# A hashed attention with a max-out FFN behind it: the first batch cut into thirds of its queries, values by even and odd dimensions of four heads, scaling straight out of PSUM, and one list of PSUM banks

## The chip, the cores and the metric

The kernel runs on one core of a Trainium2 chip. The metric is the time of one execution in microseconds of the device (us); smaller is better. One execution was also taken by the hardware profiler, and all views of the profile come from that one.

## What is computed

Four batches of eight heads, 768 positions, 64 dimensions. Each query and key gets a bucket of six bits (the signs of six projections); a query attends only to the keys of its own bucket. The heads' outputs side by side are the 512 columns of `x`, which goes through three matrices, a maximum, and a fourth matrix.

```python
q_bits = (einsum('bhsd,dk->bhsk', q, proj) > 0)          # k the same
mask = q_bucket[:, :, :, None] == k_bucket[:, :, None, :]
scores = where(mask, q @ k.T / sqrt(64), -1e9)
attn = exp(scores - max); attn = attn / (sum(attn) + 1e-9)
x = (attn @ v).transpose(0, 2, 1, 3).reshape(3072, 512)
h = maximum(maximum(x @ w1, x @ w2), x @ w3)             # 512 -> 768
out = h @ w_out                                          # 768 -> 512
```

## The kernel before

The bits stand as extra rows (plus or minus a half) under the 64 rows of each transposed head in a tile `S`, so that one matmul over 70 or 72 rows gives the score with the mask in it, and exp with a bias gives nearly zero where buckets differ.

A *unit* is 768 columns of scores: two matmuls of 128 keys by 384 queries (`scores`, L255) into one of two PSUM buffers, and one exp on ScalarE (L257) into one of 18 tiles `AT`. There are 192 units, 48 a batch. Six units make one head for one half of the queries. The program is one loop over units `u`, written out by hand, and every engine works through its own queue in that order: scores of unit u+1, then what the table `at` holds for u (`when(u, ...)`: preparation of later heads, loads), then one group of the FFN if one is waiting, then values and sums that are due.

- Preparation of batch 0 goes by *pairs* of heads. Loads of four pairs go out at the start on SP. For each pair there are four transposes on TensorE (`pair_turn`, L111), four copies to SBUF on VectorE (`pair_keep`, L117), four placings into `S` on GpSimd (`pair_place`, L122), one hash (`pair_hash`, L133: eight matmuls in fp32), the bits on VectorE (L137), and four small DMAs on SP that put the bits under the heads (L142), two a head. Pair 0 has its own shorter way (`first_place`, `first_hash`, `first_bits`: L147, L153, L158). Pairs 1 to 3 are turned at units 1 to 4, 8 to 15 and 17 to 20, and needed at units 12, 24 and 30.
- Later batches go by *quads* of four heads, turned by VectorE (L176), narrowed by GpSimd (L181), placed and hashed by L187 to L207.
- Values (`values`, L281): for a group of two heads and half of the queries, 24 matmuls of 32 columns of V, four side by side in the four 32-column strips of the array, 385 columns of `AT` each (the last is a column of ones, for the sum of V). Six such rounds fill one bank of its own. Sums (L308, L337) are the same with ones as weights.
- `far` copies the bank to SBUF (`avs`, L330), makes the reciprocals (L291 to L294), spreads them over partitions by GpSimd copies (L343 to L347), and scales six units later (L351). `near` scales out of PSUM (L314), for two groups of batch 0.
- FFN of a half of the queries: 18 first-layer groups of four matmuls (L366; L370 and L372 on VectorE) and six second-layer groups (L399, L403), one group a unit. The halves of batch 0 enter at units 40 and 57.
- PSUM: two score buffers of two banks, one bank for values, three for everything else. Weights and V are loaded by GpSimd's DMA queue: w1, w2, w3 and w_out at units 1, 9, 22 and 30, V of quad 1 at unit 14.

Of the kernel before, what the change touches and what calls it, by code (L numbers as in the profile page):

```python
# [17 lines left out]
def kernel(  # L18
# [12 lines left out]
    nc = tc.nc  # L31
# [9 lines left out]
    NPAIR = B * HPAIR  # L41
# [5 lines left out]
    UPG = NM  # L47
# [5 lines left out]
    NAT = 18  # L53
    LAG = 1

# [8 lines left out]
    avs_pool = ctx.enter_context(tc.tile_pool(name="avspool", bufs=5))  # L64
# [6 lines left out]
    av_ps = ctx.enter_context(tc.tile_pool(name="av_ps", bufs=1, space=bass.MemoryType.PSUM))  # L71
    ms_ps = ctx.enter_context(tc.tile_pool(name="ms_ps", bufs=3, space=bass.MemoryType.PSUM))
# [7 lines left out]
    at_tiles = [konst.tile([P, 2, HALF + 2], FP16, name=f"AT{i}", tag=f"AT{i}") for i in range(NAT)]  # L80
# [3 lines left out]


# [22 lines left out]
    def pair_turn(pi, side, hd, mp):  # L108
        n = nat[pi].rearrange("p (s h w) -> p s h w", s=2, h=2)
        for i in range(MH):  # L110
            nc.tensor.transpose(mp[:, i * P : (i + 1) * P], n[:, side, hd, i * P : (i + 1) * P], iden[:])  # L111
        return mp

    def pair_keep(pi, side, hd, mp):
        if pi not in t32:
            t32[pi] = t32_pool.tile([P, 2, S], FP32, tag="T32", name="T32")
        nc.vector.tensor_copy(t32[pi][:, side, hd * HALF : (hd + 1) * HALF], mp[:, 0:HALF])  # L117
# [6 lines left out]
    def pair_group(pi, side, hd):  # L124
        mp = ms_ps.tile([P, 512], FP32, tag="ms", name="mp")
        pair_keep(pi, side, hd, pair_turn(pi, side, hd, mp))

    def pair_hash(pi):
        bp = ms_ps.tile([P, 512], FP32, tag="ms", name="bp")
        for side in (1, 0):  # L130
            for hd in range(2):
# [3 lines left out]
        t32.pop(pi)  # L135
        bits = b_pool.tile([P, HALF], BF16, tag="bits", name="bits")
        nc.vector.tensor_scalar(out=bits[:], in0=bp[:, 0:HALF], scalar1=0.0, scalar2=0.5,  # L137
                                op0=AluOp.is_gt, op1=AluOp.subtract)
        for hd in range(2):
            for side in (1, 0):  # L140
                g = 2 * side + hd
                nc.sync.dma_start(s_of[pi][D : D + NBITS, g, :].rearrange("b (c n) -> b c n", c=2),  # L142
                                  bits[Q * g : Q * g + 2 * NBITS, :])
# [40 lines left out]

# [4 lines left out]

    def quad_hash(g):  # L190
        bp = ms_ps.tile([P, 512], FP32, tag="ms", name="bp")
        ts = [t32.pop((side, g)) for side in range(2)]
        for u in range(2):
            for side in range(2):
                for j in range(2):
# [5 lines left out]
                                op0=AluOp.is_gt, op1=AluOp.subtract)  # L201

# [9 lines left out]
    def v_tile(g):  # L212
        t = vo_pool.tile([P, 4, NM * D], FP16, tag="vo", name="vo")
        for x in range(4):
            v_at[4 * g + x] = (t, x)
        return t

    def load_v(g):
        b, h0 = divmod(4 * g, H)
        nc.gpsimd.dma_start(v_tile(g)[:], v[b, h0 : h0 + 4].rearrange("h (p c) d -> p h (c d)", p=P))  # L220

    def load_weights(i):
        t, w = ((w_sb[0], moe_w1), (w_sb[1], moe_w2), (w_sb[2], moe_w3), (wout_sb, moe_w_out))[i]
        nc.gpsimd.dma_start(t[:], w.rearrange("(c p) f -> p c f", p=P))


    groups = [(b, qh, jj) for b in range(B) for qh in range(2) for jj in range(HPAIR)]
    groups[0:8] = [(0, g % 2, g // 2) for g in range(4)] + [(0, g // 2, 2 + g % 2) for g in range(4)]
    NU = len(groups) * UPG
    UPB = NU // B  # L230
    xts, avs_of, av_of, sm_of = {}, {}, {}, {}


    def unit_of(u):
        g, n = divmod(u, UPG)
        if g < 4:
            hd, n = divmod(u % (2 * UPG), UPG)
            return 2 * (g // 2) + n // MH, hd, n % MH
        return g, n // MH, n % MH

    def place_of(g, hd, kp):
        if g < 4:
            return (g // 2) * 2 * UPG + hd * UPG + (g % 2) * MH + kp
        return g * UPG + hd * MH + kp

    def scores(u):
        g, hd, kp = unit_of(u)
        b, qh, jj = groups[g]
        hh = b * H + 2 * jj + hd
        (qn, qx), (kn, kx) = where[0, hh], where[1, hh]  # L250
        nb = NBITS if b == 0 else KB
        sc = sc_ps.tile([P, 2, 512], FP32, tag="sc", name="sc")
        for j in range(2):
            m = 2 * kp + j
            nc.tensor.matmul(sc[:, j, 0:HALF], s_of[kn][0 : D + nb, kx, m * P : (m + 1) * P],  # L255
                             s_of[qn][0 : D + nb, qx, qh * HALF : (qh + 1) * HALF], start=True, stop=True)
        nc.scalar.activation(at_tiles[u % NAT][:, :, 0:HALF], sc[:, :, 0:HALF], ActFn.Exp,  # L257
                             bias=-SCALE * 0.25 * nb, scale=SCALE)

    def xt_of(g):  # L260
        b, qh, jj = groups[g]
        h = 2 * b + qh
        if h not in xts:
            xts[h] = x_pool.tile([P, NJC, HALF], FP16, tag="xT", name="xT")
        return xts[h][:, jj, :]

    def at_of(g, m, hd):
        return at_tiles[place_of(g, hd, m // 2) % NAT][:, m % 2, :]

# [3 lines left out]
    def values(g):  # L273
        b, qh, jj = groups[g]
        av = av_ps.tile([P, 512], FP32, tag="av", name="av")
        for m in range(NM):
            for hd in range(2):
                vt, x = v_at[b * H + 2 * jj + hd]
                c = block_of(b, m)
                for w in range(2):  # L280
                    nc.tensor.matmul(av[hd * D + w * Q : hd * D + (w + 1) * Q, 0 : HALF + 1],  # L281
                                     vt[:, x, c * D + w * Q : c * D + (w + 1) * Q],
                                     at_of(g, m, hd)[:, 0 : HALF + 1], start=(m == 0), stop=(m == NM - 1))
        return av

    def inverse(o, sm):
        ys = ys_pool.tile([P, HALF], FP32, tag="ys", name="ys")
        rr = small.tile([P, HALF // Q], FP32, tag="rr", name="rr")  # L290
        nc.vector.transpose(ys[:], sm[:, 0:HALF])  # L291
        nc.vector.tensor_scalar(out=rr[:], in0=ys[:, 0:HALF:Q], scalar1=EPS * S, scalar2=None, op0=AluOp.add)
        nc.vector.reciprocal(rr[:], rr[:])
        nc.vector.transpose(o, rr[:].unsqueeze(2).to_broadcast((P, HALF // Q, Q)))  # L294


    def near(g):
        avs = []

        def part_values():  # L300
            avs.append(values(g))

        def part_sums():
            av = avs[0]
            sm = ms_ps.tile([P, 512], FP32, tag="ms", name="sm")
            for m in range(NM):
                for r in range(4):
                    nc.tensor.matmul(sm[Q * r : Q * (r + 1), 0:HALF], ones[:, :], at_of(g, m, r // 2)[:, 0:HALF],  # L308
                                     start=(m == 0), stop=(m == NM - 1))
            sv = small.tile([P, 2], FP32, tag="sv", name="sv")  # L310
            rc = rb_pool.tile([P, 2, HALF], FP32, tag="rb", name="rb")
            inverse(rc[:, 0, :], sm)
            nc.vector.tensor_scalar(out=sv[:, 0:1], in0=av[:, HALF : HALF + 1], scalar1=EPS, scalar2=None, op0=AluOp.mult)
            nc.vector.scalar_tensor_tensor(out=xt_of(g), in0=av[:, 0:HALF], scalar=sv[:, 0:1], in1=rc[:, 0, :],  # L314
                                           op0=AluOp.add, op1=AluOp.mult)

        return part_values, part_sums


    def far(gs):  # L320
        avs, sms, sb = [], [], []

        def part_values(i):
            if not sb:
                sb.append(small.tile([P, 2], FP32, tag="sv", name="sv"))
                sb.append(rb_pool.tile([P, 2, HALF], FP32, tag="rb", name="rb"))
            sv = sb[0]
            av = values(gs[i])
            avs.append(avs_pool.tile([P, HALF + 4], FP32, tag="avs", name="avs"))
            nc.vector.tensor_copy(avs[i][:, 0 : HALF + 1], av[:, 0 : HALF + 1])  # L330
            nc.gpsimd.tensor_scalar_mul(sv[:, i : i + 1], avs[i][:, HALF : HALF + 1], EPS)  # L331

        def part_sums():
            sms.append(ms_ps.tile([P, 512], FP32, tag="ms", name="sm"))
            for m in range(NM):
                for r in range(4):
                    nc.tensor.matmul(sms[0][Q * r : Q * (r + 1), 0:HALF], ones[:, :],  # L337
                                     at_of(gs[r % 2], m, r // 2)[:, 0:HALF], start=(m == 0), stop=(m == NM - 1))

        def invert():  # L340
            rb = sb[1]
            inverse(rb[:, 0, :], sms[0])
            nc.gpsimd.tensor_copy(rb[:, 1, :], rb[:, 0, :])  # L343
            for p0 in (0, D):
                nc.gpsimd.tensor_copy(rb[p0 + Q : p0 + D, 0, :], rb[p0 : p0 + Q, 0, :])  # L345
            for p0 in (0, D):
# [260 lines left out]
```

## Time and profile before

| | |
|---|---|
| median of three runs | 283.51 us (282.56 to 285.82) |
| span of the profiled execution | 280.6 us (its time outside the span is not recorded) |
| TensorE, weight loads, VectorE, ScalarE, GpSimd busy | 270.2, 145.9, 177.3, 166.2, 106.9 us |
| granted TensorE clock, mean | 0.998 |
| first scores, first FFN matmul, end of the last matmul | 8.5, 52.6, 277.1 us |

A group line of the profile reads: line, engine, operation, tiles, shapes, count, then busy time and mean duration in ns. A matmul's duration holds its passage through the array; how fast matmuls follow one another is read from their starts. A line of the time line reads: start, length, engine, line, what, count, and in brackets how long the engine was idle before and what ended that. A line by stretch reads: from, to, length, then the busy time (and count) of TensorE, its weight loads, VectorE, ScalarE, GpSimd, the granted clock, the share of the DMA engines and GB/s.

### The profile page before, as it was taken

What the parts mean: (1) busy time and instruction counts of PE and PEld (TensorE: products, weight loads), DVE (VectorE), ACT (ScalarE), POOL (GpSimd) and SP (SyncE); (2) the same over time, 40 slices, a digit from 0 to 9 for tenths busy, and PEclk for the clock granted to TensorE, in tenths of its full rate; (3) what the DMA queues carried; (4) which work ended last, traced back from release to release, by engine and by line L of the source; (5) the groups of instructions that cost most, each with busy time, mean ns of one, the idle gap of its engine ahead of it and who ended that gap; (6) DMA issues with size and microseconds to landing.
All of it is one profiled execution on the core that took longest, in us unless ns stands there. A gap on an engine that the chain in (4) does not pass through costs nothing.

```text
span 280.6 us, 6405 instructions
## 1 busy us (share of the span) xinstructions
PE 270.2 (96%) x2482; PEld 145.9 (52%) x2482; DVE 177.3 (63%) x383; ACT 166.2 (59%) x220; POOL 106.9 (38%) x201
## 2 busy tenths in 40 slices
PE   8899989899999999999999999999999999999994
PEld 4344433454555554555555554555555555555552
DVE  3755786786536594796536594896536673568580
ACT  2686676763858484764858484864858485910102
POOL 3455958153119096543118096633021120303000
PEclk9999999999999999999999999999999999999999
DMA  7998879974117439672117349772020001200303
GB/s 231 320 183 165 127 133 230 245 101 105 42 42 200 101 50 232 180 148 70 30 70 183 85 67 225 206 122 63 1 77 37 2 1 40 75 2 0 114 0 112
DMA packets 21877, 30.99 MB, mean 110 GB/s; under 512 B 2632, under 2 KB 17368, under 8 KB 21848
## 3 DMA queue, kind: packets, MB, share of 16 engines
q0 software_dynamic: 8640, 12.59, 24.9%
q1 hardware_dynamic: 12776, 17.49, 21.7%
q10 hardware_dynamic: 432, 0.52, 0.6%
q8 instruction: 19, 0.31, 0.5%
q14 instruction: 10, 0.08, 0.1%
HBM read 25.17 MB, written 6.29 MB: 112 GB/s over the span
## 4 chain that ended last, share of the span: by engine, by line
PE 87%; DVE 6%; ACT 2%; issue 2%; DMA 1%; POOL 0%; DVEq 0%; ACTq 0%
PE l L366 31%; PE sc L255 21%; PE av L281 12%; PE l L399 10%; PE sm L337 5%; PE bp L197 3%; ACT AT L257 2%; PE mp L111 2%; PE wp L438 1%; DVE ht L372 1%; PE bp L133 1%; PE bp L153 1%; PE sm L308 1%; DMA out_dram<-osb 1%; DVE rb L294 1%
## 5 line engine op out<-in xcount | busy, mean ns | idle before, releaser
L257 ACT ACTIVATE AT<-sc 128x768 f16<-128x768 f32 x192 | 153.4, 813 | 78.2 <-PE sc L255 78.0
L366 PE MATMUL l<-xT,w_sb 128*128 128x384 f16 x576 | 113.2, 326 | 0.7 <-DVE ht L372 0.6
L255 PE MATMUL sc<-S 72*128 72x384 bf16 (+1 forms) x384 | 93.1, 326 | 3.8 <-ACT AT L257 3.0
L366 PEld LDWEIGHTS <-w_sb 128*128 128x128 f16 x576 | 55.9, 97 | 39.1 <-issue 1.2
L372 DVE TENSOR_TENSOR ht<-ht,l 128x384 f16<-128x384 f16 x96 | 52.4, 546 | 17.0 <-PE l L366 13.8
L255 PEld LDWEIGHTS <-S 72*128 72x128 bf16 (+1 forms) x384 | 35.0, 98 | 40.1 <-issue 15.6
L331 POOL TENSOR_SCALAR sv<-avs 128x1 f32<-128x1 f32 x30 | 6.4, 213 | 95.8 <-DVE avs L330 95.7
L330 DVE COPY avs<-av 128x385 f32<-128x385 f32 x30 | 16.8, 560 | 38.3 <-PE av L281 38.3
L281 PE MATMUL av<-AT,vo 128*32 128x385 f16 x768 | 37.3, 327 | 0.0
L399 PE MATMUL l<-wout_sb,ht 128*128 128x512 f16 x138 | 36.5, 379 | 0.4 <-DVE ht L372 0.4
L370 DVE CAST ht<-l 128x384 f16<-128x384 f32 x48 | 26.2, 547 | 16.0 <-PE l L366 15.2
L403 ACT COPY osb<-l 128x512 f32<-128x512 f32 x23 | 13.4, 582 | 27.2 <-PE l L399 27.2
L281 PEld LDWEIGHTS <-vo 128*32 128x32 f16 x768 | 18.6, 96 | 16.9 <-issue 8.7
L181 POOL TENSOR_SCALAR T<-T 128x768 bf16<-128x768 f32 x24 | 21.5, 894 | 13.3 <-DVE T L176 11.9
L176 DVE STREAM_TRANSPOSE T<-nat 128x384 f32<-128x384 f32 x48 | 26.2, 558 | 0.0
L399 PEld LDWEIGHTS <-ht 128*128 128x128 f16 x138 | 13.3, 97 | 13.8 <-DVE ht L372 1.8
L351 DVE SCALAR_TENSOR_TENSOR xT<-avs,sv,rb 128x384 f16<-128x384 f32 x30 | 19.7, 656 | 0.0
L337 PE MATMUL sm<-AT,ones 128*32 128x384 f16 x360 | 17.2, 326 | 0.0
L343 POOL COPY rb<-rb 128x384 f32<-128x384 f32 x15 | 7.5, 503 | 24.0 <-DVE rb L294 24.0
L122 POOL TENSOR_SCALAR S<-T 64x768 bf16<-64x768 f32 (+1 forms) x17 | 12.8, 754 | 8.0 <-DVE T L117 6.9
L347 POOL COPY rb<-rb 32x384 f32<-32x384 f32 x30 | 15.0, 500 | 1.5
L345 POOL COPY rb<-rb 32x384 f32<-32x384 f32 x30 | 15.0, 499 | 1.5
(47 smaller groups left out, 136.5 us busy)
## 6 DMA issues: line engine op xcount, KB each, us to landing
out_dram<-osb SPq DMA_DIRECT2D x23, 256.0 KB
S<-T SPq DMA_DIRECT2D x48, 96.0 KB
vo<-in_v_dram POOLq DMA_DIRECT2D x8, 384.0 KB, 6.1
nat<-in_k_dram POOLq DMA_DIRECT2D x16, 192.0 KB, 3.6
nat<-in_q_dram POOLq DMA_DIRECT2D x16, 192.0 KB, 5.8
w_sb<-in_moe_w_dram POOLq DMA_DIRECT2D x3, 768.0 KB, 9.7
nat<-in_k_dram SPq DMA_DIRECT2D x10, 192.0 KB
nat<-in_q_dram SPq DMA_DIRECT2D x8, 192.0 KB
```

The source lines that it names most:

```text
L176: nc.vector.transpose(t32[name][:, u, half * HALF : (half + 1) * HALF], i_)
L181: nc.gpsimd.tensor_scalar(out=t16[name][:, u, :], in0=t32[name][:, u, :], scalar1=RS, scalar2=1.0, op0=AluOp.mult, op1=AluOp.mult)
L255: nc.tensor.matmul(sc[:, j, 0:HALF], s_of[kn][0 : D + nb, kx, m * P : (m + 1) * P], s_of[qn][0 : D + nb, qx, qh * HALF : (qh + 1) * HALF], ...
L257: nc.scalar.activation(at_tiles[u % NAT][:, :, 0:HALF], sc[:, :, 0:HALF], ActFn.Exp, bias=-SCALE * 0.25 * nb, scale=SCALE)
L281: nc.tensor.matmul(av[hd * D + w * Q : hd * D + (w + 1) * Q, 0 : HALF + 1], vt[:, x, c * D + w * Q : c * D + (w + 1) * Q], at_of(g, m, hd) ...
L330: nc.vector.tensor_copy(avs[i][:, 0 : HALF + 1], av[:, 0 : HALF + 1])
L337: nc.tensor.matmul(sms[0][Q * r : Q * (r + 1), 0:HALF], ones[:, :], at_of(gs[r % 2], m, r // 2)[:, 0:HALF], start=(m == 0), stop=(m == NM ...
L351: nc.vector.scalar_tensor_tensor(out=xt_of(gs[i]), in0=avs[i][:, 0:HALF], scalar=sv[:, i : i + 1], in1=rb[:, i, :], op0=AluOp.add, op1=Alu ...
L366: nc.tensor.matmul(ps[:, 0:HALF], w_sb[wi][:, jc, fb * P : (fb + 1) * P], xt[:, jc, :], start=(jc == 0), stop=(jc == NJC - 1))
L370: nc.vector.tensor_copy(hts[fb][:], ps[:, 0:HALF])
L372: nc.vector.tensor_tensor(out=hts[fb][:], in0=hts[fb][:], in1=ps[:, 0:HALF], op=AluOp.max)
L399: nc.tensor.matmul(ps[:, 0:DM], hts[fb][:, tb * P : (tb + 1) * P], wout_sb[:, fb, :], start=(fb == 0), stop=(fb == NFB - 1))
```

## The change

- **Thirds.** Batch 0 is cut into three chunks of 256 queries; the other batches keep two of 384. A unit of a third is three matmuls of 128 keys by 256 queries, and a head has two such units. The order starts with heads 0 and 1 in chunks 0 and 1, then heads 2 to 7 of chunk 0, heads 2 to 7 of chunk 1, then chunk 2. So head 2 (pair 1) comes at unit 8, pair 2 at unit 12, pair 3 at unit 16. Turns of pairs 1 to 3 are set at units 1 to 3, 4 to 7 and 8 to 11, hashes at 4, 8 and 12; the second half of each pair's queries is placed later (units 10, 14, 18).
- **Values.** A burst is four heads of one chunk: one bank of sums, one of even dimensions, one of odd ones, 24 matmuls each. Its value weights are every second element of V. The rows of w1, w2 and w3 are loaded in an order that fits.
- **Scaling** reads PSUM, with the reciprocals already in the right partitions; the avs copies and the GpSimd copies go. The sum of V is taken once for each quad and side.
- **Banks.** Four banks in one list, taken and given back in order. There are 26 AT tiles.
- **Order.** Bursts of chunks 0 to 2 are split over three units, the others are in one piece; quad hashes come one unit later, outside the burst. FFN of a chunk enters two units after its last piece: chunk 0 at unit 24. Chunk 0's FFN goes matrix by matrix. The loads of w1, w2, w3 and w_out are at units 0, 7, 11 and 28, V of quad 1 at unit 5; the keys of quad 2 are loaded at unit 9 and no longer at the start. Two of pair 0's copies go from VectorE to ScalarE.

```diff
-    groups = [(b, qh, jj) for b in range(B) for qh in range(2) for jj in range(HPAIR)]
...
+    chunks = [(b, w * n, w) for b in range(B) for w in (THIRD if b == 0 else HALF,)
+              for n in range(S // w)]
...
+    order = [(0, 0), (1, 0), (0, 1), (1, 1)] + [(c, h) for c in range(2) for h in range(2, H)]
+    order += [(c, h) for c in range(2, NCH) for h in range(H)]
...
+            for m in range(m0, m1):
+                cb = block_of(b, m)
+                for x in range(4):
+                    nc.tensor.matmul(av[Q * x : Q * (x + 1), 0:n], v_at[2 * b + i][:, x, cb * D + side : (cb + 1) * D : 2],
+                                     weights_of(c, 4 * i + x, m)[:, 0:n], start=(m == 0), stop=(m == NM - 1))
...
+                nc.vector.scalar_tensor_tensor(out=xt_of(c)[:, 2 * i + side, 0:w], in0=av[:, 0:w],
+                                               scalar=sv_of[b, i, side][:], in1=rb[0][:, 0:w], op0=AluOp.add, op1=AluOp.mult)
...
+        if c == 0:
+            jobs = [(fb, wi) for wi in range(3) for fb in range(NFB)]
...
-        load_quad(1, 2, range(4), nc.sync)
...
+        pair_keep(0, 1, 1, mk1, nc.scalar)
...
-        for pi, us, uh in ((1, (1, 2, 3, 4), 6), (2, (8, 9, 14, 15), 16), (3, (17, 18, 19, 20), 21)):
+        for pi, us, uh, ul in ((1, (1, 1, 2, 3), 4, 10), (2, (4, 5, 6, 7), 8, 14), (3, (8, 9, 10, 11), 12, 18)):
             for u, (side, hd) in zip(us, ((1, 0), (1, 1), (0, 0), (0, 1))):
                 when(u, pair_group, pi, side, hd)
                 if hd == 1:
-                    for par in range(2):
-                        when(u, pair_place, pi, side, par)
+                    when(u, pair_place, pi, side, 0)
+                    when(u if side == 1 else ul, pair_place, pi, side, 1)
             when(uh, pair_hash, pi)
-        when(14, load_v, 1)
-        for n, u in enumerate((1, 9, 22, 30)):
+        when(5, load_v, 1)
+        for n, u in enumerate((0, 7, 11, 28)):
             when(u, load_weights, n)
-        for u, side, g in ((8, 0, 2), (23, 1, 3), (25, 0, 3)):
+        for u, side, g in ((9, 1, 2), (12, 0, 2), (23, 1, 3), (25, 0, 3)):
...
+            for n, f in enumerate(pieces):
+                u = d + n if c < 3 else d
...
+            ffn_at.setdefault(last_of[c] + 2, []).append(c)
```

More of the change, by code (lines that the diff above doesn't have):

```diff
@@ L241, in place_of @@
[L241 to L268, printed above, removed]
+        if i == 3:
+            nc.gpsimd.dma_start(wout_sb[:], moe_w_out.rearrange("(c p) f -> p c f", p=P))
+            return
+        w = (moe_w1, moe_w2, moe_w3)[i]
+        nc.gpsimd.dma_start(w_sb[i].rearrange("p (i u) f -> p i (u f)", u=2),
+                            w.rearrange("(i p u) f -> p i (u f)", p=P, u=2))
@@ new lines, with parts_of @@
+    chunks = [(b, w * n, w) for b in range(B) for w in (THIRD if b == 0 else HALF,)
+              for n in range(S // w)]
+    NCH = len(chunks)
+    def parts_of(c):
+        return chunks[c][2] * NM // (2 * HALF)
+    order = [(0, 0), (1, 0), (0, 1), (1, 1)] + [(c, h) for c in range(2) for h in range(2, H)]
+    order += [(c, h) for c in range(2, NCH) for h in range(H)]
+    units = [(c, h, n) for c, h in order for n in range(parts_of(c))]
+    NU = len(units)
+    UPB = NU // B
+    done_at = {}
@@ L270, in block_of, with blocks @@
+    for u, (c, h, n) in enumerate(units):
+        done_at[c, h // 4] = u
+    at_free = list(range(NAT))
+    at_form = [THIRD] * NAT
+    at_of = {}
+    xts, sv_of = {}, {}
+    def blocks(t, w):
+        nb = 2 * HALF // w
+        return t[:, 0 : nb * (w + 2)].rearrange("p (n c) -> p n c", n=nb)
     def block_of(b, m):
         return 2 * (m % MH) + m // MH if b == 0 else m
[L273 to L284, printed above, removed]
@@ L288, in inverse @@
[L288 to L308, printed above, removed]
-                                     start=(m == 0), stop=(m == NM - 1))
[L310 to L317, printed above, removed]
@@ L320, in far @@
[L320 to L346, printed above, removed]
-                nc.gpsimd.tensor_copy(rb[p0 : p0 + Q, 1, :], rb[p0 + Q : p0 + D, 1, :])
-        def scale(i):
-            sv, rb = sb
-            nc.vector.scalar_tensor_tensor(out=xt_of(gs[i]), in0=avs[i][:, 0:HALF], scalar=sv[:, i : i + 1],
-                                           in1=rb[:, i, :], op0=AluOp.add, op1=AluOp.mult)
-        return part_values, part_sums, invert, [(6 + i, lambda i=i: scale(i)) for i in range(2)]
@@ new lines, with weights_of, xt_of, burst @@
+    unit_at = {e: u for u, e in enumerate(units)}
+    def weights_of(c, h, m):
+        w = chunks[c][2]
+        nb = 2 * HALF // w
+        return blocks(at_tiles[at_of[unit_at[c, h, m // nb]]], w)[:, m % nb, :]
+    def xt_of(c):
+        if c not in xts:
+            xts[c] = x_pool.tile([P, NJC, HALF], FP16, tag="xT", name="xT")
+        return xts[c]
+    def burst(c, i):
+        b, q0, w = chunks[c]
+        held = {}
+        rb = []
+        def sums(m0, m1):
+            if m0 == 0:
+                held["s"] = bank()
+            sm = held["s"][1]
+            for m in range(m0, m1):
+                for x in range(4):
+                    nc.tensor.matmul(sm[Q * x : Q * (x + 1), 0:w], ones[:, :], weights_of(c, 4 * i + x, m)[:, 0:w],
+                                     start=(m == 0), stop=(m == NM - 1))
+            if m1 == NM:
+                ys = ys_pool.tile([P, HALF], FP32, tag="ys", name="ys")
+                rr = small.tile([P, HALF // Q], FP32, tag="rr", name="rr")
+                n = w // Q
+                rb.append(rb_pool.tile([P, HALF], FP32, tag="rb", name="rb"))
+                nc.vector.transpose(ys[:, 0:w], sm[:, 0:w])
+                give(held["s"][0])
+                nc.vector.tensor_scalar(out=rr[:, 0:n], in0=ys[:, 0:w:Q], scalar1=EPS * S, scalar2=None, op0=AluOp.add)
+                nc.vector.reciprocal(rr[:, 0:n], rr[:, 0:n])
+                nc.vector.transpose(rb[0][:, 0:w], rr[:, 0:n].unsqueeze(2).to_broadcast((P, n, Q)))
+        def values(side, m0, m1):
+            if m0 == 0:
+                held[side] = bank()
+            av = held[side][1]
+            first = (b, i, side) not in sv_of
+            n = w + 1 if first else w
+            for m in range(m0, m1):
+                cb = block_of(b, m)
+                for x in range(4):
+                    nc.tensor.matmul(av[Q * x : Q * (x + 1), 0:n], v_at[2 * b + i][:, x, cb * D + side : (cb + 1) * D : 2],
+                                     weights_of(c, 4 * i + x, m)[:, 0:n], start=(m == 0), stop=(m == NM - 1))
+            if m1 == NM:
+                if first:
+                    sv_of[b, i, side] = small.tile([P, 1], FP32, tag=f"sv{side}", name="sv")
+                    nc.vector.tensor_scalar(out=sv_of[b, i, side][:], in0=av[:, w : w + 1], scalar1=EPS, scalar2=None,
+                                            op0=AluOp.mult)
+                nc.vector.scalar_tensor_tensor(out=xt_of(c)[:, 2 * i + side, 0:w], in0=av[:, 0:w],
+                                               scalar=sv_of[b, i, side][:], in1=rb[0][:, 0:w], op0=AluOp.add, op1=AluOp.mult)
+                give(held[side][0])
+                if side == 1:
+                    for h in range(4 * i, 4 * i + 4):
+                        for n in range(parts_of(c)):
+                            at_free.append(at_of[unit_at[c, h, n]])
+        return sums, values
@@ new lines, in ffn_groups, with go @@
+    def ffn_groups(c):
+        b, q0, w = chunks[c]
+        xt = xt_of(c)
+        hts, gs, l2 = {}, [], {}
+        jobs = [(fb, wi) for fb in range(NFB) for wi in range(3)]
+        if c == 0:
+            jobs = [(fb, wi) for wi in range(3) for fb in range(NFB)]
+        for fb, wi in jobs:
+            def go(fb=fb, wi=wi):
+                k_, ps = bank()
+                for jc in range(NJC):
+                    nc.tensor.matmul(ps[:, 0:w], w_sb[wi][:, jc, fb * P : (fb + 1) * P], xt[:, jc, 0:w],
+                                     start=(jc == 0), stop=(jc == NJC - 1))
+                if wi == 0:
+                    hts[fb] = h_pool.tile([P, HALF], FP16, tag="ht", name="ht")
+                    nc.vector.tensor_copy(hts[fb][:, 0:w], ps[:, 0:w])
+                else:
+                    nc.vector.tensor_tensor(out=hts[fb][:, 0:w], in0=hts[fb][:, 0:w], in1=ps[:, 0:w], op=AluOp.max)
+                give(k_)
+            gs.append(go)
```

248 lines of the change are left out of this document (118 added, 130 removed).

## The prediction

> **What bounds the kernel now.** I read the page first (busy shares, slices, chain), then the stretches of time, then the time line of the first 45 us, because the slices are uneven only there.
>
> ```profile
> PE 270.2 (96%) x2482; PEld 145.9 (52%) x2482; DVE 177.3 (63%) x383; ACT 166.2 (59%) x220; POOL 106.9 (38%) x201
> ...
> DMA  7998879974117439672117349772020001200303
> ...
> PE 87%; DVE 6%; ACT 2%; issue 2%; DMA 1%; POOL 0%; DVEq 0%; ACTq 0%
> ```
>
> TensorE is the bound and the chain runs along it; VectorE and GpSimd have room. Two lines by stretch show where TensorE is not full:
>
> ```profile
> 30.00:40.00 10.00, 8.98 (x104) 3.67 (x101) 7.08 (x15) 6.61 (x10) 6.35 (x9) 1.00 0.70 96
> ...
> 62.00:100.00 38.00, 38.00 (x374) 20.71 (x372) 21.73 (x45) 23.94 (x32) 12.28 (x27) 1.00 0.39 96
> ```
>
> The second number is TensorE's busy time. From 62 us on it is full, and the starts of its matmuls confirm it: 0.162 us apart for 384 columns, which is one L366 group of four in 0.65. Adding up the gaps between starts that exceed this, I find 7.0 us of waiting between 8.5 us (first scores) and 52.6 us (first FFN matmul), and about 1 us in all after that. So the span is a start of 52.6 us, then 224.5 us of nearly solid matmuls up to 277.1, then 3.6 us of copying out. What the change does to time is the start, plus the work left after it.
>
> In the start the heads are made ready by a long path: transpose (PE, L111), copy (DVE, L117), hash (PE, L133), bits (DVE, L137), four small DMAs on SP (L142).
>
> ```profile
> 16.44 0.85 PE L133 MATMUL bp<-T,pj 128*32 128x384 f32 x8
> ...
> 17.41 0.56 DVE L137 TENSOR_SCALAR bits<-bp 128x384 bf16<-128x384 f32 x1 [1.35 <-PE bp L133]
> ...
> 18.00 3.29 SPq L142 DMA_DIRECT2D S<-bits  x4
> ```
>
> That is pair 1 (heads 2, 3). By the trace's DMA records the two transfers of head 2 landed at 20.2 and 20.9, 4.5 us after the hash began. Head 2 is unit 12, whose exp ran at 21.6: just in time. Now the last bits of pair 3 against a weight load:
>
> ```profile
> 35.53 0.79 POOL L224 DMA_DIRECT2D w_sb<-in_moe_w_dram  x1
> ```
>
> ```profile
> 28.64 8.34 SPq L142 DMA_DIRECT2D S<-bits  x8
> ```
>
> The eight issues of the second line (0.72 each) are pairs 2 and 3. Those issued at 33.96 and 34.73 landed after 1.9 us. The one issued at 36.26, 0.73 behind the weight load, landed at 42.5, with the tail of that load (42.2 to 43.4); its packets last 0.05 us each but the first starts at 40.9. Likewise the bits issued at 29.43, just behind the load of V at 28.96, landed at 34.5 with it. Small transfers issued behind a large load land with its end.
>
> **The change, part by part.**
>
> *Work left after the first FFN matmul*, priced by spacings of this trace (0.162 for 384 columns; 0.109 for 256, from the twelve matmuls of L381: 1.47 us less the 0.27 of one, over 11). FFN of chunk 0 starts at u24, with scores up to 25 done, where before it started at u40 with scores up to 41 done.
> - Scores left: 66 of 256 columns and 288 of 384 against 300: 7.2 + 46.5 - 48.5 = +5.2.
> - First layer of batch 0: 216 x 0.109 - 144 x 0.162 = +0.3.
> - Values left: four quads of 12 rounds (a round is four matmuls side by side) at 0.109 against 12 rounds at 0.162: +3.3. Sums: 24 rounds at 0.109 against 6 at 0.162: +1.6.
> - One more quad hash is left (1.4), and four hashes leave the middle of a burst and pay the switch in and out again (0.2 each): +2.2. The gap on going into 32-column matmuls is 0.095 us and out again 0.098; batch 0 has 12 separate pieces left against 3: +1.7.
> - The wait at 251.8 us for a late scale (0.8) goes, since PSUM is scaled at once: -0.8. Next on VectorE there: transpose 0.58, two small ones 0.40, transpose 0.58, two scalings of 0.62; three banks are held for that 2.8 us, while TensorE still has the two value pieces (1.9) and two groups on the other banks. No new wait.
> - VectorE at u24 to u31: a transpose (0.56), an evacuation of 256 columns (0.42, L387) and 2.0 of burst work twice in four units make about 9.8 us against 8.7 of TensorE: +1.0 (0 to 2).
>
> Sum: +14.5, so 224.5 + 14.5 = 239.0. The removed avs copies (L330, 16.8 us) and GpSimd's rb and sv copies (L331 to L347, 44 us) lie beside a full TensorE; I price them at nothing, and their cover is TensorE itself. The added memsets (0.06 each) and the wider value weights with a step of two elements lie there too.
>
> Rounds of 256 columns are not in the trace. Lower end 0.109: the weight loads of a round are issued with the round before and take 0.097, so they still fit. Upper end 0.162, if the round does not shrink: 72 rounds, +3.8. I take the lower, as L381 has the same weight loads and gets 0.109.
>
> *The start.* Batch 0 needs pair 1 at u8 instead of u12, pair 2 at u12 instead of u24, pair 3 at u16 instead of u30. TensorE's queue is in order: while scores(8) waits for bits, the transposes of the next pair wait behind it, and ACT and the next hash behind those.
> - Pair 1: two copies of the first pair move to ACT (0.5 each, beside its 0.57 of waiting after the first exp). On DVE, eight small bits (0.56) from 7.3, then four copies (0.55) end at 15.1; hash at 15.2, bits at 16.2, SP at 16.75. Head 2's second transfer is issued at 17.7 and lands 1.9 later: scores(8) at 19.7. (w1 is out at about 11.6, and the four k loads of quad 2, taken out of its way, were 2.6 us of packets, so it is drained by then.)
> - Pair 2: its last transpose stands behind scores(8): 20.4, copy to 21.15, hash 21.2, bits 22.2 to 22.7, SP 22.75 and 23.7. But GpSimd's queue runs from the same copy: place (L122, 0.86) to 22.0, then w2 at 22.05. V of quad 1 went out at 19.6. So the bits stand 0.7 us behind a weight load, as at 36.26. With 7.0 us from the load's issue to the landing of such bits (42.5 - 35.5), scores(12) run at 29.1, instead of 25.7 with 1.9.
> - Pair 3 repeats it: copy ends 1.5 after scores(12), place, w3 at 31.4, bits behind it (k loads of quad 2 now stand between in SP's queue, 2.3 us of issues over by 28): landing 38.4, scores(16) at 38.5. The burst of the first quad lies in that wait.
> - From scores(16), four units at ACT's 0.75, then three of scores, burst piece and switch (0.33 + 0.65 + 0.19 = 1.17), and the lag to scores(25): 8.0. First FFN matmul at 46.5. Weights are in by then; w_out goes out near 50, took 11.9 us before, and is needed near 66.
>
> **Sum.** 46.5 + 239.0 + 3.6 = 289.1 us of span, against 280.6. The median of the runs shown, 283.5, is 2.9 above the profiled span, and I add the same: 292.0. In other words the start gives back 6.1 us and 14.5 us of work are still to do, since TensorE waits some 14 us in the start instead of 7.
>
> [...] The row says that the bits of 36.26 waited 4.7 us for their first packet. [...]
>
> **The rivals.**
> 1. *The bits slip past the loads* (1.9 us as at 33.96). scores(12) at 25.7, pair 3's bits issued at 29.7 land at 31.6, first FFN at 39.7: span 282.3, time 285.2. For it: the order of the w2 issue and the bits rests on 0.7 us of my walk. Against it: two loads, both ahead by the same construction.
> 2. *Faster.* The pairs are ready before TensorE asks, so that ACT alone sets the pace: 24 units at 0.75 to 0.8 from 9.0, and four burst pieces that exceed it by 0.4, plus the tiny waits of the first units (1.3 at units 0 to 4 instead of 0.8): first FFN at 34 to 35. Span 277.1, time 280.0. It turns on one thing, scores(12) not waiting; below a first FFN at 35.2 the change is faster by 1%. Against it: hash to landing took 4.5 us, and four units of ACT are 3.0.
> 3. *Rounds of 256 columns do not shrink*: +3.8 on the sum, 295.8. For it: eight instructions in 0.109 us occur nowhere. Against: the four matmuls of a round start within 10 ns.
> 4. *Only one of the two pairs is caught*: first FFN near 43, 288.5.
>
> The clock is a further unknown. The warm-up matmuls took 0.320 instead of 0.162 for the first 4 us of the run, and later no gap of TensorE reaches 1.3 us; here it idles for over 4 us before scores(12). [...]
>
> **How the numbers follow.** Likeliest, both caught: 0.42, own range 289 to 294. Rival 1: 0.23. Rival 2: 0.12. Rival 3 on top of the likeliest: 0.13. Rival 4: 0.10. The range goes from the fast side of rival 1 (first FFN at 36.5) to rival 3: 282 to 296; rival 2 and a little above are left out. One per cent of 283.5, about what a measurement can tell from no change, is 2.8: faster is below 280.7 (rival 2, 0.13), within 1% reaches to 286.3 (most of rival 1 and the slow side of rival 2, 0.22), the rest is slower (0.65).
>
> **What would show it.** In the profile after: scores waiting several us at u8, u12 and u16, for DMAs of bits; the bits of pairs 2 and 3 landing with w2 and w3; first FFN matmul (L368) at 46 and not below 40; from there to the last matmul 239 us; 256-column rounds at 0.11. If L368 starts before 36 the walk of the start is wrong; if the stretch after it is far from 239, the ledger is.

## The result, and the profile after

The changed kernel takes 302.94 us (median of four, 301.54 to 304.57) against 283.93 for the kernel before on the same chip: a ratio of 1.066, 95% interval 1.060 to 1.072. The forecast was 292.0 with a range of 282 to 296, so slower was right and the size was not. In all ratios, runs of the kernel before that lie over 1.5% above its fastest are left out. The profiled execution took 302.64 us with a span of 300.9; the table puts its marks beside the forecast's.

| us | before | forecast | after |
|---|---|---|---|
| scores of unit 8 / 12 / 16 | | 19.7 / 29.1 / 38.5 | 19.91 / 31.08 / 41.14 |
| first FFN matmul | 52.6 | 46.5 | 52.0 |
| from there to the end of the last matmul | 224.5 | 239.0 | 245.4 |
| tail; time beyond the span | 3.6; 2.9 | 3.6; 2.9 | 3.5; 2.0 |

Two things were added to the forecast: 5.5 us in the start and 6.4 after it (less 1.0 in the last row; with that, 10.9 in all). First the page of the changed kernel: busy times, the granted clock by fortieths of the span, the DMA engines, and the chain that ended last.

```profile
PE 279.8 (93%) x2722; PEld 163.9 (54%) x2722; DVE 168.6 (56%) x425; ACT 166.0 (55%) x222; POOL 61.0 (20%) x96
...
PEclk9987576999998799999999999999999999999999
...
DMA  7959698292699211374892202843001000200202
...
PE 85%; DMA 7%; DVE 3%; ACT 2%; issue 1%; POOL 1%; SPq 1%; DVEq 0%; ACTq 0%
```

GpSimd is down from 106.9 us to 61.0, as the removed copies say. TensorE is busy 9.6 us longer, DMAs have gone from 1% of the chain to 7%, and the clock, 0.998 before, is 0.5 in places. The same stretches as ahead of the change, and two more (TensorE's busy time is the second number, the clock the third from the end):

```profile
30.00:40.00 10.00, 7.88 (x95) 4.64 (x95) 3.67 (x10) 3.24 (x4) 3.19 (x4) 0.64 0.73 132
40.00:52.90 12.90, 11.31 (x122) 6.36 (x126) 3.30 (x10) 7.19 (x10) 0.00 (x0) 0.60 0.93 188
62.00:100.00 38.00, 33.89 (x409) 22.31 (x402) 20.84 (x65) 22.24 (x30) 12.66 (x20) 0.94 0.87 167
93.00:103.00 10.00, 5.95 (x62) 3.03 (x62) 1.87 (x6) 2.50 (x4) 0.00 (x0) 0.66 0.84 127
```

The stretch from 62 to 100 us was solid before (38.00 of 38.00) and now has a hole of 4.1 us; its DMA share is 0.87 against 0.39. The time line of TensorE shows where it waited; these are all the scores that waited for bits:

```profile
31.08 0.80 PE L284 MATMUL sc<-S 70*128 70x256 bf16 x3 [5.85 <-DMA S<-bits]
41.14 1.44 PE L284 MATMUL sc<-S 70*128 70x256 bf16 x6 [2.18 <-DMA S<-bits]
97.29 0.80 PE L284 MATMUL sc<-S 72*128 72x384 bf16 x2 [4.05 <-DMA S<-bits]
```

They are units 12, 16 and 60. The first two were forecast, the third was not. Unit 8 ran when forecast (19.91 for 19.7), but the trace puts its wait of 1.89 us down to GpSimd, whose placings of pair 1 ended at 19.77; the bits landed at 19.78. The working had only the bits, so that one is right partly by luck. For the first two, the time line of GpSimd has the weight loads w2 and w3:

```profile
22.72 0.75 POOL L235 DMA_DIRECT2D w_sb<-in_moe_w_dram  x1
...
34.08 0.75 POOL L235 DMA_DIRECT2D w_sb<-in_moe_w_dram  x1
```

and that of SP the bits (the first line ends with pair 2, issued from 23.95 to 26.25 us; the second is pair 3):

```profile
16.85 10.12 SPq L155 DMA_DIRECT2D S<-bits  x8
...
35.32 3.06 SPq L155 DMA_DIRECT2D S<-bits  x4
```

Both pairs stand 1.2 us behind a load, and both land within a microsecond of that load's end (by the trace's DMA records w2 at 30.6 and its pair's bits at 30.3 to 31.5, w3 at 41.0 and its pair's at 40.5 to 41.6). That is the forecast's likeliest case. The third wait is on the chain of the stretch from 86 to 104 us:

```profile
88.99 8.16 DMA S<-bits
...
97.29 0.80 PE sc L284 x2
```

One small transfer of the bits of quad 3, issued at 88.99, needs 8.2 us; in the kernel before, the same transfers needed 2.2 to 3.0. What lies directly ahead of it is SP's own work, above all the placings of quad 3 (`S<-T`):

```profile
78.21 2.57 SPq L199 DMA_DIRECT2D S<-T  x4
...
81.53 2.81 SPq L199 DMA_DIRECT2D S<-T  x4
87.42 3.02 SPq L219 DMA_DIRECT2D S<-bits  x4
```

By the trace's DMA records these eight landed 5.0 us after their issue at first and 12.1 at last (95.6), and the first packet of the bits started only at 93.6, behind nearly all of theirs. From 76.5 to 88.0 us GpSimd had issued twelve loads, of quads 4 and 5 and of V, and from 82 to 93 us packets of these loads and of the placings lie side by side, with a DMA share of 1.04 to 1.21 (stretches from 85.0 to 95.3); with most of the loads held back (below), the placings landed after 3.1 to 5.2 us. In the kernel before, the same loads of quads 4 and 5 stand behind the copies that the change removes. GpSimd's time line before,

```profile
84.25 1.04 POOL L345 COPY rb<-rb 32x384 f32<-32x384 f32 x2
85.35 1.04 POOL L347 COPY rb<-rb 32x384 f32<-32x384 f32 x2
86.34 1.70 POOL L170 DMA_DIRECT2D nat<-in_k_dram  x3
```

and after:

```profile
79.37 2.24 POOL L183 DMA_DIRECT2D nat<-in_k_dram  x4
81.60 2.18 POOL L183 DMA_DIRECT2D nat<-in_q_dram  x4
...
88.85 0.56 POOL L183 DMA_DIRECT2D nat<-in_k_dram  x1
```

The program sets these loads at unit 60 and on, and the bits of quad 3 at unit 51, in both kernels. The copies waited for VectorE's reciprocals, and so kept GpSimd's queue near TensorE's place: before, all but one of the eight loads of quad 4 went out from 86.3 us, when the exps were at unit 67, long after the bits of quad 3 (69.1 us, unit 52). In the changed kernel they went out from 79.4, when the exps were at unit 47, and the placings and bits (unit 51, now 87.4 us, as more of the FFN lies ahead of it) met them. (Of the kernel before: six units are two heads, not one, for a half of the queries; it is from this that unit 60 is the first of quad 3.)

### The profile page after: what moved, and what is told of

It reads as the page before. It is cut to its first block, busy times and chain, and to the rows that moved or that the text cites. A ratio compares the mean times of both kernels' runs of the same rounds, so it can differ in the third digit from the quotient of the medians.

```text
span 300.9 us, 6822 instructions
## 1 busy us (share of the span) xinstructions
PE 279.8 (93%) x2722; PEld 163.9 (54%) x2722; DVE 168.6 (56%) x425; ACT 166.0 (55%) x222; POOL 61.0 (20%) x96
## 4 chain that ended last, share of the span: by engine, by line
PE 85%; DMA 7%; DVE 3%; ACT 2%; issue 1%; POOL 1%; SPq 1%; DVEq 0%; ACTq 0%
PE ms L368 29%; PE sc L284 21%; PE ms L339 10%; PE ms L402 9%; DMA S<-bits 6%; PE ms L317 6%; PE ms L208 3%; ACT AT L292 2%; PE ms L146 2%; PE ms L119 2%; PE ms L441 1%; DVE S L171 1%; DMA out_dram<-osb 1%; PE ms L166 1%; POOL S L133 1%
## 5 line engine op out<-in xcount | busy, mean ns | idle before, releaser
L368 PE MATMUL ms<-xT,w_sb 128*128 128x384 f16 (+1 forms) x648 | 116.6, 309 | 0.0
L284 PE MATMUL sc<-S 72*128 72x384 bf16 (+1 forms) x432 | 98.5, 322 | 16.2 <-DMA S<-bits 12.1
L374 DVE TENSOR_TENSOR ht<-ht,ms 128x384 f16<-128x384 f16 (+1 forms) x108 | 54.5, 505 | 32.3 <-PE ms L368 29.7
L284 PEld LDWEIGHTS <-S 72*128 72x128 bf16 (+1 forms) x432 | 40.5, 101 | 50.1 <-issue 27.2
L372 DVE CAST ht<-ms 128x384 f16<-128x384 f32 (+1 forms) x54 | 27.4, 508 | 38.4 <-PE ms L368 37.7
L339 PE MATMUL ms<-AT,vo 128*32 128x385 f16 (+3 forms) x864 | 37.0, 316 | 0.0
L402 PE MATMUL ms<-wout_sb,ht 128*128 128x512 f16 x138 | 36.0, 378 | 0.0
L406 ACT COPY osb<-ms 128x512 f32<-128x512 f32 x23 | 13.4, 581 | 27.2 <-PE ms L402 27.2
L324 DVE STREAM_TRANSPOSE ys<-ms 128x384 f32<-128x384 f32 (+1 forms) x18 | 9.7, 539 | 21.7 <-PE ms L317 21.7
L346 DVE SCALAR_TENSOR_TENSOR xT<-ms,sv,rb 128x384 f16<-128x384 f32 (+1 forms) x36 | 20.0, 570 | 2.4 <-PE ms L339 1.2
L317 PE MATMUL ms<-AT,ones 128*32 128x384 f16 (+1 forms) x432 | 21.1, 336 | 0.0
L317 PEld LDWEIGHTS <-ones 128*32 128x32 f16 x432 | 11.1, 103 | 9.5 <-issue 6.8
```

Of the source, the lines that this page charges most:

```text
L284: nc.tensor.matmul(views[j], s_of[kn][0 : D + bits, kx, m * P : (m + 1) * P], s_of[qn][0 : D + bits, qx, q0 : q0 + w], start=True, stop=True)
L317: nc.tensor.matmul(sm[Q * x : Q * (x + 1), 0:w], ones[:, :], weights_of(c, 4 * i + x, m)[:, 0:w], start=(m == 0), stop=(m == NM - 1))
L339: nc.tensor.matmul(av[Q * x : Q * (x + 1), 0:n], v_at[2 * b + i][:, x, cb * D + side : (cb + 1) * D : 2], weights_of(c, 4 * i + x, m)[:, 0 ...
L346: nc.vector.scalar_tensor_tensor(out=xt_of(c)[:, 2 * i + side, 0:w], in0=av[:, 0:w], scalar=sv_of[b, i, side][:], in1=rb[0][:, 0:w], op0=A ...
L368: nc.tensor.matmul(ps[:, 0:w], w_sb[wi][:, jc, fb * P : (fb + 1) * P], xt[:, jc, 0:w], start=(jc == 0), stop=(jc == NJC - 1))
L372: nc.vector.tensor_copy(hts[fb][:, 0:w], ps[:, 0:w])
```

## Experiments

All ratios are to the kernel before, run on the same chip (283.4 to 283.7 us). The theory: the change costs 14.5 us of work, as forecast; the bits of pairs 2 and 3 are caught behind w2 and w3; the bits of quad 3 are held up by loads that GpSimd issues too early, which slow SP's queue; and every such wait is made longer by the half clock (0.5) around it. The rivals: the bits are late on SP's own queue; the lost time is the clock's, not the waits'; the 256-column work costs more than its ledger.

**The weights behind the bits.** GpSimd reads a few of pair 3's bits before it issues w2 and w3, so that both loads follow the bits.

```diff
+    gate = konst.tile([P, 8], BF16, name="gate")
...
+        if i == 1:
+            nc.gpsimd.tensor_copy(gate[D : D + NBITS, 0:8], s_of[3][D : D + NBITS, 1, S - 8 : S])
...
-        for n, u in enumerate((0, 7, 11, 28)):
+        for n, u in enumerate((0, 13, 13, 28)):
```

> The changed kernel with w2 and w3 loaded only after the last bits of pair 3 have landed (a tiny GpSimd copy that reads those bits stands before the loads). If bits that stand behind a large load are what holds the start, the bits of pairs 2 and 3 land about 2 us after their issue, scores of unit 12 run near 27 us instead of 31.4 and of unit 16 near 33 instead of 41.1, the first FFN matmul comes at 39 to 42 us instead of 52.0, and the time falls from 302.9 to 290 to 293. If the path transpose, copy, hash, bits is too long by itself, the first FFN matmul stays above 48 and the time above 298.

294.46 us (293.64 to 295.74), ratio 1.040 [1.035, 1.046]: 8.5 us less than the changed kernel, and 1.5 above what was expected. GpSimd's time line has both loads behind the read,

```profile
32.83 0.18 POOL L233 COPY gate<-S 6x8 bf16<-6x8 bf16 x1 [5.32 <-DMA S<-bits]
32.97 1.49 POOL L238 DMA_DIRECT2D w_sb<-in_moe_w_dram  x2
```

and TensorE's has units 12 and 16 nearly six and ten microseconds earlier:

```profile
25.19 0.49 PE L287 MATMUL sc<-S 70*128 70x256 bf16 x3 [1.84 <-DMA S<-bits]
...
31.56 0.82 PE L287 MATMUL sc<-S 70*128 70x256 bf16 x6 [0.97 <-DMA S<-bits]
```

The bits are issued at 22.18 and 28.53 and used three microseconds later. So the loads were the delay. The first FFN matmul comes at 40.85, 11.1 earlier; of that, 2.1 is lost again, since from there to the last matmul it takes 247.5: the wait at unit 60 is still there.

**GpSimd held back.** After each burst's reciprocals GpSimd copies eight of them into a scratch tile. The copy has no other use than to make GpSimd wait there, as the removed copies did.

```diff
                 nc.vector.transpose(rb[0][:, 0:w], rr[:, 0:n].unsqueeze(2).to_broadcast((P, n, Q)))
+                nc.gpsimd.tensor_copy(step[:, :], rb[0][:, 0:8])
```

> The changed kernel with one tiny GpSimd copy of eight columns of the reciprocals behind each burst, so that GpSimd's queue can no longer run ahead of the bursts. If the wait of unit 60 at 93 to 97 us comes from loads of quads 4 and 5 that GpSimd now issues about 20 us early, those loads go out after 95 us, the bits of quad 3 land within 3 us, the wait and the half clock after it go, and the time falls by 6 to 8 us, to 295 to 297, with the first FFN matmul left at 52. If the bits of quad 3 are late for another reason (the hash one unit later, the slow start), the wait stays and the time moves by less than 2.

296.64 us (294.02 to 296.76), ratio 1.045 [1.039, 1.052]: 6.3 us less. GpSimd's time line now has one load of quad 4 ahead of unit 60 and the others after the next burst:

```profile
84.87 0.19 POOL L330 COPY step<-rb 128x8 f32<-128x8 f32 x1 [4.62 <-DVE AT L291]
85.83 0.60 POOL L184 DMA_DIRECT2D nat<-in_k_dram  x1 [0.77 <-PE ms L370]
98.88 0.19 POOL L330 COPY step<-rb 128x8 f32<-128x8 f32 x1 [12.45 <-DVE sv L346]
99.39 1.64 POOL L184 DMA_DIRECT2D nat<-in_k_dram  x3 [0.32 <-issue]
```

The placings of quad 3 now land 3.1 to 5.2 us after their issue and its bits 2.1 to 3.0, and no scores wait for bits after the start. The first FFN matmul is at 52.38 and the last matmul ends at 291.40, 239.0 between them, as the forecast's ledger has it. Eighteen copies of 0.19 us gain 6.3 us by making their engine late.

**Both.** The two edits together.

> Both edits: weights after the bits, and GpSimd paced by the bursts. If the two waits are separate causes, the gains add: first FFN matmul at 39 to 42, 239 us from there to the last matmul, time 283 to 287, about that of the kernel before. If a third thing is at work (rounds of 256 columns, the split bursts), it stays above 290.

285.98 us (285.61 to 286.74), ratio 1.010 [1.006, 1.015]: 17.0 us less than the changed kernel, against 8.5 and 6.3 for each alone. They add, and a little more: with the weights gated alone, unit 60 waited 5.65 us instead of 4.05, and that goes too. First FFN matmul 42.62, last matmul 281.04: 238.4 of work left. What remains of the loss is the work, with a start that gives back 10 us of it.

**The clock filled.** Matmuls of zeros into a spare bank, 10, 30, 18 and 24 of them, ahead of scores 8, 12, 16 and 60, so that TensorE isn't idle while it waits.

```diff
+        fills = {8: 10, 12: 30, 16: 18, 60: 24}
...
+            if u + 1 in fills:
+                fill(fills[u + 1])
```

> The changed kernel with idle TensorE filled: 10, 30, 18 and 24 matmuls of zeros in front of the scores of units 8, 12, 16 and 60. They wait for nothing and give nothing, and leave every transfer as it is. If the idle time halves the clock, and the half clock then stretches the start, the granted clock stays near 1.0, the first FFN matmul comes 2 to 5 us earlier in spite of the added work, the 6.8 us of half clock at 95 us go, and the time falls to 294 to 300. If the half clock costs nothing (it lies in waiting), the time stays at 303 or grows by up to 4.

301.5 us (300.15 to 302.83), ratio 1.063 [1.056, 1.070]; the intervals of this and of the changed kernel overlap, and it lies between the two outcomes that were expected. Two of its stretches:

```profile
20.00:30.00 10.00, 8.72 (x62) 5.33 (x59) 2.77 (x5) 3.02 (x4) 4.36 (x6) 1.00 0.96 159
...
93.00:103.00 10.00, 8.86 (x103) 5.53 (x103) 2.72 (x11) 3.26 (x5) 0.39 (x1) 1.00 0.86 146
```

The clock is full in both (0.68 and 0.66 before the fill). It changes little: unit 12 runs at 30.5 and unit 16 at 40.9 instead of 31.1 and 41.1, since both still wait for the same loads. From unit 60 to unit 72 it takes 14.2 us instead of 16.2, so the half clock cost 2 us there, though unit 60 itself comes later than without the fill (99.1 for 97.3). The fill also failed to hold the clock behind unit 16, where it was half from 43.0 to 53.2. The waits are the cause, and the clock is what they cost on top.

**The bits on another queue.** The four small DMAs of each pair are issued from ScalarE's queue instead of SP's.

```diff
-                nc.sync.dma_start(s_of[pi][D : D + NBITS, g, :].rearrange("b (c n) -> b c n", c=2),
+                nc.scalar.dma_start(s_of[pi][D : D + NBITS, g, :].rearrange("b (c n) -> b c n", c=2),
```

> The changed kernel with the twelve transfers of bits of pairs 1 to 3 issued from ScalarE's queue instead of SP's; the loads stay where they are. If small transfers stand behind the load inside the DMA engines, whatever queue they come from, they land as late as before, units 12 and 16 run within 2 us of 31.9 and 42.0, and the time stays within 3 of 303. If the delay is one of SP's own queue, or engines take turns between queues, unit 12 runs near 27 and the time falls towards 292.

One run, 303.48 us. The time line of ScalarE's queue for pair 2, then TensorE's for unit 12 (w2 was issued at 24.82):

```profile
26.05 3.08 ACTq L155 DMA_DIRECT2D S<-bits  x4
```

```profile
32.40 0.80 PE L284 MATMUL sc<-S 70*128 70x256 bf16 x3 [4.00 <-DMA S<-bits]
```

From the first issue to the scores it takes 6.4 us, against 7.1 from SP. By the page's table of queues 216 packets have moved from queue q1 to q10, so another queue was really used. So for the pairs the delay isn't SP's queue: it is met from either. (At unit 60 the bits came behind the placings of SP's own queue, their first packet at 93.6; this run leaves those bits on it.)

**Three chunks first.** With both cures, the order of units also changes: heads 0 and 1 go through all three chunks before head 2, so that pair 1 is needed at unit 12, pair 2 at 16, pair 3 at 20. FFN of chunk 0 then enters at unit 28.

```diff
-    order = [(0, 0), (1, 0), (0, 1), (1, 1)] + [(c, h) for c in range(2) for h in range(2, H)]
-    order += [(c, h) for c in range(2, NCH) for h in range(H)]
+    order = [(c, h) for h in range(2) for c in range(3)] + [(c, h) for c in range(3) for h in range(2, H)]
+    order += [(c, h) for c in range(3, NCH) for h in range(H)]
```

> Both edits of the run before (weights after the bits, GpSimd paced), and heads 0 and 1 go through all three chunks before head 2, so that pair 1 is needed at unit 12, pair 2 at 16 and pair 3 at 20, each four units later; chunk 0 is then complete at unit 23 and its FFN enters at unit 28. If what is left of the start (2.2, 1.9 and 1.3 us before units 8, 12 and 16 with both edits) is the path transpose to bits set against four units of exp, these three waits nearly go, the first FFN matmul stays near 42 us though it is now unit 28, and the time falls by 3 to 5 us against 286.0, to 281 to 283, faster than before. If those waits come from somewhere else, they only move, and the time stays at 286.

280.5 us (279.73 to 282.94), ratio 0.990 [0.986, 0.993]: faster than the kernel before, by 2.9 us or 1%. Its page:

```profile
PE 269.6 (97%) x2722; PEld 159.2 (57%) x2722; DVE 167.4 (60%) x425; ACT 165.1 (59%) x222; POOL 64.6 (23%) x115
...
PEclk9999999999999999999999999999999999999999
...
PE 93%; DVE 3%; ACT 2%; issue 1%; DMA 1%; DVEq 0%; ACTq 0%
```

No slice is short of clock, and DMA is back at 1% of the chain. The start has no wait for bits left; the waits that remain are for ScalarE's exps (0.2 to 0.8 each), so that ScalarE sets the pace, as in the forecast's rival 2. First FFN matmul 37.64, last matmul 274.83: 237.2 of work.

**The order alone**, without the two cures:

> The changed kernel with only the order of the last version: heads 0 and 1 through all three chunks first; weights and quads are loaded as the change has them, and GpSimd is not paced. If both collisions are causes of their own, four more units of exp before each pair (3 us) cannot hide a load of 5 to 7 us: bits of one pair at least still land with a load, the bits of quad 3 still stand behind the early loads of quads 4 and 5 (4 us and half clock), and the time is 289 to 297. If the order alone was the fault, it is 282 to 285.

299.04 us (298.04 to 300.15), ratio 1.055 [1.049, 1.062]. Four units more of time for each pair are not enough, as w2 (20.55) and w3 (24.87) still go out ahead of pair 3's bits (25.25). It came 2 us above what was expected; the stretch of its start shows half clock throughout, which is a likely reason (that it is the whole of it is not shown):

```profile
30.00:40.00 10.00, 6.50 (x54) 3.32 (x45) 1.87 (x5) 3.96 (x6) 0.00 (x0) 0.50 1.09 236
```

The order is worth 5.5 us on top of the cures (285.98 to 280.5) and 3.9 without them.

**Halves again.** Both cures, but batch 0 in halves of 384 queries as in the kernel before; values by even and odd, scaling and banks stay as changed.

```diff
-    chunks = [(b, w * n, w) for b in range(B) for w in (THIRD if b == 0 else HALF,)
+    chunks = [(b, w * n, w) for b in range(B) for w in (HALF,)
...
-                u = d + n if c < 3 else d
+                u = d + n if c < 2 else d
```

> Both edits, and batch 0 cut into halves again, with all else of the change kept (values by even and odd dimensions, scaling out of PSUM, one list of banks, bursts split in batch 0). Pairs are needed at units 12, 18 and 24 and the FFN enters at unit 34. If the thirds are what costs, the waits of the start go, and the time is 280 to 284. If values, scaling or banks cost something of their own, it stays at 286 or above.

285.84 us (285.33 to 288.45), ratio 1.010 [1.005, 1.015]: not the 280 to 284 of a cost that lies in the thirds, but about the 286 of the other case. From the first FFN matmul to the last it takes 230.2 us (50.5 to 280.71), but the first is only 2 us earlier than in the kernel before, and the start has waits of up to 1.2 us for ScalarE and 10.2 us of half clock:

```profile
14.54 0.49 PE L288 MATMUL sc<-S 70*128 70x384 bf16 x2 [1.06 <-ACT AT L296]
...
37.89 0.98 PE L288 MATMUL sc<-S 70*128 70x384 bf16 x4 [1.24 <-ACT AT L296]
```

So the values, the scaling and the banks don't pay by themselves here. What they cost the run doesn't tell: 230.2 is 5.7 us more than the 224.5 of before, but the FFN enters six units earlier (34 instead of 40), so six units of scores (about 1.9 us at 0.162 a matmul) and the values of two more groups (another 1.9) still lie behind it. Thirds in the first order gain nothing on halves either (285.98, both cures); what pays is the early FFN of the thirds once nothing waits for bits: 280.5 against 285.8.

## Why the prediction was right and wrong, step by step

- **Pairs 2 and 3 caught behind w2 and w3: right.** Both issued 1.2 us behind a load, both landing within a microsecond of its end; gating the loads gave 8.5 us. Rivals 1 and 4 are out by the traces, and rival 2 appears only in the kernel with the new order.
- **The work left, 239.0: right.** 239.0 with GpSimd held back, 238.4 with both cures. The sum is confirmed, most of its terms were not measured one by one, and that it fits to the tenth is luck. Rival 3 is settled: 24 matmuls of 256 columns, six rounds of values, take 0.84 us with the last one's own duration, and the starts of their rounds are 0.10 apart. The lower end, 0.109, was the one to take.
- **"I price them at nothing, and their cover is TensorE itself": wrong, the step that failed.** As busy time the copies of GpSimd did cost nothing. But it was they that kept GpSimd's loads behind VectorE. Without them the loads of quads 4 and 5 run ahead and slow SP's placings of quad 3 to as much as 12.1 us, the bits behind these take 8.2 us, and unit 60 waits 4.05 us. It cost 6.3 us (by the run with GpSimd held back), nearly all of the 6.4 that the forecast lacked after the first FFN matmul. The working itself has loads hold up small transfers, one part further on. It looked for this among the loads that the diff moves in the list, and not among those that move because their queue is freed.
- **The clock, which has no term in the sum: missing there.** From unit 16 to the first FFN matmul it took 10.9 us where 8.0 was forecast; 40.6 to 50.9 ran at half clock. With the clock half for only 3.4 us of it, in the run with the weights behind the bits, it took 9.3 (31.56 to 40.85), and at full clock, in the kernel with three chunks first (the same work from unit 20, 29.84 to 37.64), 7.8. So these +2.9 are the clock. Another 2 us went behind unit 60, within the 6.3 above.
- **scores(12) and scores(16): mis-sized.** w2 went out at 22.72 (forecast 22.05; TensorE was at half clock from 20.2 to 23.6) and the scores came 8.4 us behind it, where the working took 7.0 from the one load of before; V of quad 1, issued at 19.72, was still being moved until 24.8. That is +2.0. From there to unit 16 it took 10.1 instead of 9.4: +0.7. With the +2.9 of the clock, this is the 5.5 of the start.
- **Time beyond the span, 2.9: it was 2.0** for the changed kernel; -0.9. Every run that is recorded with its span lies 1.7 to 1.8 above it, so by an estimate from these the 2.9 held some 1.1 us by which the profiled execution of the kernel before was faster than the median.

## What to carry to other kernels

When a change takes work off an engine that also issues DMAs, read what stands behind that work in its queue, and which transfers the freed loads will meet: idle as the work was, it paced the loads, and a copy of 0.19 us put back in its place was worth 6.3 us. Small transfers that the bounding engine waits for should be issued ahead of large loads, or the loads made to depend on them, which was worth 8.5 us here. And price a wait of TensorE by more than its length: the wait of 4 us at unit 60 cost 2 us more through the clock behind it.

## What the runs showed of the hardware

*Small transfers beside large loads.* In the start, pair 2's bits were issued from 23.95 and nothing else stood in their queue, but their first packet started at 28.1, near the end of w2's packets (24.2 to 29.7); they landed 5.3 to 6.3 us after their issue, where pair 1's, whose first packet started at 18.4 with 251 of w1's 256 already started, needed 1.9 to 2.1. From ScalarE's queue it was 4.2 to 5.9 (issued from 26.05, scores at 32.40). At unit 60 packets of GpSimd's loads and of SP's placings lie side by side from 82 to 93 us, and the bits follow the placings in SP's queue. At which stage the small transfers were held back no run shows.

*The clock.* Half clock came in stretches of 3.4 us or multiples (3.4, 6.8, 10.2, and 20.5 in the order alone), also behind a stretch in which TensorE was busy for 1.76 of 3.40 us. The changed kernel by stretches of 3.4 us:

```profile
37.20:40.60 3.40, 1.76 (x47) 0.97 (x35) 1.45 (x5) 1.15 (x2) 0.00 (x0) 1.00 1.03 212
40.60:44.00 3.40, 2.60 (x12) 1.62 (x13) 0.00 (x0) 1.84 (x3) 0.00 (x0) 0.51 1.04 219
44.00:47.40 3.40, 3.20 (x33) 1.52 (x32) 0.00 (x0) 2.69 (x4) 0.00 (x0) 0.50 1.11 217
47.40:50.90 3.50, 3.50 (x48) 1.75 (x48) 1.91 (x6) 1.33 (x2) 0.00 (x0) 0.50 1.10 215
```

A stretch that is busy for 1.76 of 3.40 us is followed by half clock, and it stays half, though the next two are busy for 2.60 and 3.20, until one is busy throughout. In the run with both cures 2.18 of 3.40 was followed by half clock as well; in the kernel with three chunks first, 2.56 of 3.41 (29.09 to 32.51) was not, but in the run with the weights behind the bits neither was 1.84 of 3.41 (21.52 to 24.93), so the busy share alone doesn't decide it. With GpSimd held back, one stretch busy throughout (46.89 to 50.31) was not enough to end the half clock: from 40.0 to 52.9, busy for 11.88 of 12.90 us, the clock was 0.50. At unit 16 a wait of 2.18 us, up to 41.14, went with 10.2 us of half clock from 40.6 on. The same start did not bring the same clock: the program is the same up to unit 12 in the runs with the weights gated and with both cures, but only the second had half clock from 20.0 to 23.4, and it took 7.0 us from unit 8 to unit 12 where the first took 5.9.

The ends of the matmuls are modelled, so the busy times are not exact. Two more things stay open: the start of the run with the clock filled, where half clock came in spite of the fill, and how much of the 17.0 us of both cures is the clock and how much the waits.
